# Five moves in the first two segments of a fused recurrence, MLP and MoE kernel: a buffer of its own and a sooner load for the first triangles' columns, weight conversions behind the first triangles, router steps and early scans in another place

## The chip, the cores and the metric

The kernel runs on one core of a Trainium2 chip. The metric is the time of one execution on the device, in microseconds (us); lower is better. TensorE (PE) does the matrix multiplications and the transpositions that go through PSUM, VectorE (DVE), ScalarE (ACT) and GpSimd (POOL) do elementwise work, and SyncE (SP) issues most of the DMA transfers. Each engine executes its own instructions in order, and waits for others through semaphores.

## The reference

Three stages follow one another: a recurrence over 768 time steps for 4 x 8 heads of 40 dimensions, an MLP with a squared ReLU on its 3072 x 320 output, and a mixture of 8 experts, of which each token takes one, with 768 places per expert.

```python
for t in range(S):                               # S = 768, 32 heads, D = 40
    y[:, :, t] = einsum('bhd,bhde->bhe', rt, state)
    Sa = einsum('bhde,bhe->bhd', state, at)
    state = state * wt[:, :, None, :] - einsum('bhd,bhe->bhde', Sa, bt)
    state = state + einsum('bhd,bhe->bhde', vt, kt)
...
x = np.maximum(x @ w_in, 0.0)                    # x 3072x320, w_in 320x2048
x = (x * x) @ w_out                              # w_out 2048x320
...
logits = x @ w_gate                              # 320x8
expert_idx = np.argmax(logits, axis=1)
h = np.maximum(np.einsum('ecd,edf->ecf', disp, w1), 0.0)   # disp 8x768x320
y = np.einsum('ecf,efd->ecd', h, w2)
out[i] = gate_w[i] * y[expert_idx[i], pos[i]]
```

## The kernel before

**The recurrence** (class `Rwkv`) is cut into 12 segments `s` of 64 steps, and each segment into two chunks `c` of 32 steps. Within a chunk the 32 dependent steps are turned into a triangular system. For one segment:

- `scale(s)` loads the decays `w_d` and the keys `kb_d`, takes running products of the decays (two scans, to `rq_r` and back into `w_d`, L127 and L140), multiplies `kb_d` by the first (L158), loads the columns `rq_a` (L163), multiplies them by the second (L167), and `place` writes them by DMA into the tiles `a` (L177). `products` has the scans; `g` is a copy of a few of their columns.
- `lower(s, c)` multiplies `kb_d` with `rq_a` on PE (tile `pa`), and ACT and DVE copy and mask the result (`sad_ab`, `am`, and its transposition to `a`, L213).
- `invert(s)` transposes the triangles on DVE (`solve_al`, L220) and then inverts them on POOL in 31 steps of two operations, `tmp` and `tl` (L333).
- `inverted(s)` transposes the inverse on DVE (`solve_tf`, L242) and adds its two halves into `tt`.
- `steps(s)` scans `wl` and transposes it to `rt` and `qt`. The state update of a chunk follows: `pr`, `psa`, `psd`, `ppq`, `pn` (the new state) and `py`, `pz` on PE, `zv` on DVE, and copies on ACT.

The tiles `solve_al` and `solve_tf` share one buffer (the tag before the dot in their names). So do `rq_r` and the columns `rq_a`, both named `rq16`: the load of `rq_a` therefore starts after the last reader of `rq_r`.

**The MLP** (class `Mlp`) runs beside the recurrence. Its float64 weights come as pairs of 32-bit words and are converted: `load_out(n)` makes one of 16 tiles of `w_out` (from the `stage` tiles; `ao`, `woh`, `lo`), `load_in(fp, k)` one of 20 blocks of `w_in` (`raw`, then `a`, `wi_hi`, `wi_lo`; the blocks of the third row group have `mh` and `ml`, and go to `wi_mx` by DMA). `from_double` is one ACT operation and three on DVE (L565 to L567); the remainder `lo`, `wi_lo` or `ml` is a subtraction in `less`, which for a few tiles is on POOL (L572) and else on DVE (L574). A block `raw` takes one of two tags with a few buffers. `routers` multiplies the gate into `w_out` (`ptg`, `wt`, `pog`, `wogl`). `add_y` turns a finished segment into `x_hi`, `x_lo` and `x_mx`, and `bursts` runs the MLP itself on it: `pl` (L494), `g`, `gh`, `gl` (L715), `acc` (L677).

**What sets the order.** The main loop goes through the segments and chunks, and each chunk through eight slots. After each slot, `mlp(n)` takes `n` pieces of the queue (first router steps, then bursts); the numbers stand in `FIRST` for segment 0, `SECOND` for segment 1 and `SLOTS` from segment 2 on. A scheduler orders the instructions of each engine by priority; within `high_priority` blocks they go ahead of the others. `issue_after(i)` puts what is issued in it behind instruction `i`: `behind(n)` behind the first `n` additions of the state update (`sums`), and `gated()` behind the list `gate` while `steady` holds, which is from segment 2 on. `gate` is the last `solve_al` and the `x_mx` of `add_y`. Before the loop stand `scale(0)`, four calls of `load`, `lower(0)` and `invert(0)`, the other calls of `load`, `steps(0)` and `scale(1)`.

## Time and profile before

| | |
|---|---|
| median of the runs | 1017.08 us (3 runs, 1012.47 to 1021.44) |
| profiled execution | 1013.06 us |
| its span | 1011.2 us |
| mean granted TensorE clock | 0.986 |
| busy PE / DVE / ACT / POOL | 877.8 / 744.1 / 620.0 / 540.0 us |
| chain that ended last | PE 31%, POOL 26%, DVE 13%, DMA 11%, issue 11%, ACT 5% |
| segments 0 to 11 | up to about 660 us; after it the rest of the MLP and the experts |

The profiled execution is 4.0 us shorter than the median. "Busy" counts the time in which an engine executes something; 31% in the chain's row says that this share of the span lies on the chain of work that was followed back from the last instruction, on that engine. The two lines of the inversion on POOL (`tl` and `tmp`, L333) are 13% and 12% of the span there.

### The profile page before, as it was taken

The numbers are of one execution on the slowest core, as the hardware profiler recorded it, in microseconds if no ns is written. First come the engines' busy times: TensorE is split into PE (matmuls) and PEld (weight loads), VectorE is DVE, ScalarE is ACT, GpSimd is POOL, SyncE is SP. The second block draws the span as 40 slices with busy tenths as digits, with TensorE's granted clock in tenths as the row PEclk, the third lists the DMA queues.
The fourth block names the chain that finished last, engine by engine and source line by source line (L and its number), as shares of the span: only waits on it lengthen the run. The fifth ranks groups of instructions, "written<-read, shape, count | busy, mean of one in ns | idle before, by whom it ended". The sixth has DMA issues, their size and how long they took to land.

```text
span 1011.2 us, 38777 instructions
## 1 busy us (share of the span) xinstructions
PE 877.8 (87%) x15962; PEld 824.2 (82%) x15962; DVE 744.1 (74%) x1657; ACT 620.0 (61%) x1618; POOL 540.0 (53%) x863
## 2 busy tenths in 40 slices
PE   1066666999998999999999999998899999999992
PEld 1055555898898999989998898998899889999992
DVE  7879698478777687878788775646569778888860
ACT  2144555566665767667666676664775577777750
POOL 4885759278777768787877878300000332323310
PEclk9999999999998999999999999999999999999997
DMA  7583653856655656656565655541882777777710
GB/s 218 167 286 93 179 168 115 289 150 174 175 173 158 181 162 187 176 175 177 177 183 176 187 164 150 144 133 56 262 257 76 225 208 235 219 230 233 232 48 10
DMA packets 91213, 177.17 MB, mean 175 GB/s; under 512 B 16490, under 2 KB 46828, under 8 KB 90061
## 3 DMA queue, kind: packets, MB, share of 16 engines
q1 hardware_dynamic: 87196, 164.99, 55.8%
q0 software_dynamic: 2880, 8.98, 2.8%
q8 instruction: 129, 2.11, 0.9%
q10 hardware_dynamic: 944, 0.57, 0.3%
q14 instruction: 64, 0.52, 0.2%
HBM read 138.52 MB, written 16.24 MB: 153 GB/s over the span
## 4 chain that ended last, share of the span: by engine, by line
PE 31%; POOL 26%; DVE 13%; DMA 11%; issue 11%; ACT 5%; SPq 1%; POOLq 0%; DVEq 0%; ACTq 0%
POOL tl L333 13%; POOL tmp L333 12%; PE pl L494 8%; PE acc L677 7%; PE upl L494 5%; PE uacc L1205 4%; DMA out_dram<-uo,room 4%; DMA xg<-x_dram,room 2%; DMA wol<-wol 1%; DVE rq_r L127 1%; PE pn L336 1%; DMA kb_d<-in_kb_dram 1%; PE ppq L336 1%; DVE solve_al L220 1%; DVE solve_tf L242 1%
## 5 line engine op out<-in xcount | busy, mean ns | idle before, releaser
L333 POOL TENSOR_TENSOR tmp<-solve_al,tl 128x126 f32<-128x126 f32 (+22 forms) x372 | 218.8, 588 | 74.5 <-DVE solve_al L220 46.3
L333 POOL TENSOR_TENSOR tl<-tl,tmp 128x126 f32<-128x126 f32 (+22 forms) x372 | 224.1, 602 | 29.0
L677 PE MATMUL acc<-woh,gh 128*128 128x328 f32 x384 | 127.9, 339 | 2.2 <-ACT x L739 2.2
L677 PE MATMUL acc<-wol,gh 128*128 128x328 f32 x384 | 119.3, 317 | 2.1 <-DMA wol<-wol 1.8
L494 PE MATMUL pl<-x_hi,wi_hi 128*128 128x256 f32 x384 | 116.0, 302 | 0.0
L1213 POOL DMA_INDIRECT xg<-x_dram,room x30 | 32.6, 1087 | 155.7 <-DVE x_lo L509 69.5
L494 PE MATMUL pl<-x_lo,wi_hi 128*128 128x256 f32 x384 | 109.3, 285 | 6.5 <-DVE x_lo L509 6.2
L494 PE MATMUL pl<-x_hi,wi_lo 128*128 128x256 f32 x384 | 108.9, 284 | 0.0
L1289 POOL DMA_INDIRECT out_dram<-uo,room x30 | 33.7, 1125 | 133.1 <-DVE uo L1278 79.4
L700 ACT ACTIVATE g<-pl 128x512 f32<-128x512 f32 x96 | 57.4, 598 | 72.3 <-PE pl L494 67.8
L715 DVE TENSOR_TENSOR gl<-g,gh 128x512 fp32r<-128x512 f32 x96 | 67.2, 700 | 37.0 <-ACT gh L704 36.5
L677 PE MATMUL acc<-woh,gl 128*128 128x328 f32 x384 | 90.0, 315 | 0.6 <-issue 0.6
L494 PEld LDWEIGHTS pl<-x_lo,wi_hi 128*128 128x128 f32 x384 | 73.3, 191 | 6.5 <-DVE x_lo L509 6.5
L677 PEld LDWEIGHTS acc<-woh,gh 128*128 128x128 f32 x384 | 72.9, 190 | 6.8 <-ACT x L739 2.4
L1205 PE MATMUL uacc<-w2h,hh 128*128 128x320 f32 x240 | 75.1, 313 | 3.4 <-ACT wi_hi L1161 2.7
L494 PEld LDWEIGHTS pl<-x_hi,wi_hi 128*128 128x128 f32 x384 | 73.0, 190 | 3.6
L677 PEld LDWEIGHTS acc<-wol,gh 128*128 128x128 f32 x384 | 73.4, 191 | 2.6 <-DMA wol<-wol 2.0
L1205 PE MATMUL uacc<-w2h,hl 128*128 128x320 f32 x240 | 74.5, 310 | 0.0
L1205 PE MATMUL uacc<-w2l,hh 128*128 128x320 f32 x240 | 74.3, 309 | 0.0
L494 PEld LDWEIGHTS pl<-x_hi,wi_lo 128*128 128x128 f32 x384 | 73.3, 191 | 0.4 <-issue 0.4
L336 PE MATMUL pa<-kb_d,rq_a 40*32 40x64 f32 x1536 | 31.3, 241 | 46.4 <-DVE rq_a L167 45.5
L336 PEld LDWEIGHTS pa<-kb_d,rq_a 40*32 40x32 f32 x1536 | 27.3, 123 | 50.6 <-DVE rq_a L167 45.7
(264 smaller groups left out, 2685.8 us busy)
## 6 DMA issues: line engine op xcount, KB each, us to landing
wol<-wol SPq DMA_DIRECT2D x96, 328.0 KB
w<-in_w_dram SPq DMA_DIRECT2D x30, 640.0 KB
w<-in_w_dram SPq DMA_DIRECT2D x30, 512.0 KB
zv<-in_vt_dram SPq DMA_DIRECT2D x48, 208.0 KB
kb_d<-in_kb_dram SPq DMA_DIRECT2D x24, 320.0 KB
tk<-in_tok_dram SPq DMA_DIRECT2D x24, 320.0 KB
rx<-rt SPq DMA_DIRECT2D x192, 40.0 KB
zk<-tk SPq DMA_DIRECT2D x48, 160.0 KB
```

The costliest lines, as they stand in the source:

```text
L127: nc.vector.tensor_tensor_scan(out=rf[:, ::-1], data0=w[:rows, 1:][:, ::-1], data1=seed, initial=0.0, op0=ALU.mult, op1=ALU.add)
L220: i = nc.vector.transpose(out=al.rearrange("p s t -> p (s t)"), in_=self.ab.rearrange("p s c h -> p s (c h)")[:, :, None].to_broadcast([12 ...
L242: nc.vector.transpose(out=tf.rearrange("p t u c h -> p (t u c h)"), in_=tl[:, :, :, None].to_broadcast([128, C, C // 2, 2]))
L333: self.last = f(*a, **k).ins
L336: self.tc.keep_in_program_order(self.nc.tensor.matmul(*a, **k))
L494: tc.keep_in_program_order(tc.nc.tensor.matmul(out, lhsT=a, rhs=b, start=n == 0, stop=n == len(seq) - 1))
L677: self.tc.keep_in_program_order(self.nc.tensor.matmul(*a, **k))
L700: nc.scalar.activation(g, pl, AF.Relu)
L715: i = self.nc.vector.tensor_tensor(out=p[4], in0=g, in1=gh.bitcast(F32), op=ALU.subtract)
L1205: self.tc.keep_in_program_order(self.nc.tensor.matmul(*a, **k))
L1213: nc.gpsimd.indirect_dma_start(out=xg[:, 0:DX], out_offset=None, in_=self.x1, in_offset=bass.IndirectOffsetOnAxis(ap=self.idx[2 * j + t], ...
L1289: self.nc.gpsimd.indirect_dma_start(out=self.out, out_offset=bass.IndirectOffsetOnAxis(ap=self.to[:, n:n + 1], axis=0), in_=o[:, t], in_of ...
```

## The change

The diff has five parts. (1) The columns `rq_a` of segment 0 get the tag `solve`, which `solve_al` has, and their load is issued inside the first step of `scale(0)`. (2) All calls of `load` stand behind the first `lower` and `invert`, and the first DVE operation of each conversion is issued after the first `solve_al` (`hold`). (3) `solve_tf` of segments 0 and 1 is not put behind the state update any more. (4) All 34 router pieces are taken in segment 0; before, six were left for segment 1, and they have other slots now. (5) `steady` holds from segment 1 on.

```diff
@@ -149,7 +149,10 @@
             nc.sync.dma_start(out=w[BY_COL[j]], in_=src["wd"][s, j])
         for j in range(2):
             nc.sync.dma_start(out=kb[BY_COL[j]], in_=src["kb"][s, j])
-
+        x = None
+        if s == 0:
+            x = self.tile([128, NC, 16, C], f"rq16.a{s}", 1, tag="solve")
+            nc.sync.dma_start(out=x[:ROWS].rearrange("p c n t -> p (c n t)"), in_=src["ad"][s])
         yield
         pr = self.products(w, 16, ROWS, s)
         with self.gated():
@@ -159,8 +162,9 @@
         g = self.tile([128, 16], f"g64.{s}", 2)
         nc.vector.tensor_copy(g[:ROWS], r[:ROWS, :, 0])
         self.pre[s] = [g, [None] * NC, None]
-        x = self.tile([128, NC, 16, C], f"rq16.a{s}", 1)
-        nc.sync.dma_start(out=x[:ROWS].rearrange("p c n t -> p (c n t)"), in_=src["ad"][s])
+        if x is None:
+            x = self.tile([128, NC, 16, C], f"rq16.a{s}", 1)
+            nc.sync.dma_start(out=x[:ROWS].rearrange("p c n t -> p (c n t)"), in_=src["ad"][s])
         yield
         q = next(pr)
         yield
@@ -238,7 +242,7 @@
 
         nc, tl = self.nc, self.tl
         tf = self.tile([128, C, 2, NC, H], f"solve.tf{s}", 1)
-        with self.behind(1):
+        with self.behind(s > 1):
             nc.vector.transpose(out=tf.rearrange("p t u c h -> p (t u c h)"),
                                 in_=tl[:, :, :, None].to_broadcast([128, C, C // 2, 2]))
         tt = self.tile([128, C, NC, H], f"tt.{s}", 1)
@@ -538,6 +542,7 @@
         self.gl = w.tile([128, NFT, NEXP], F32R, name="wogl")
         self.wg = w.tile([128, 3, NEXP], F32, name="wg")
 
+        self.hold = self.first = None
         self.tops = [w.tile([128, self.NT], F32R, name=f"tops{i}") for i in range(2)]
         self.turned = 0
         for t in self.tops:
@@ -562,7 +567,8 @@
         V = nc.vector
         af = a.bitcast(F32)
         nc.scalar.activation(af, up.bitcast(F32), AF.Abs, scale=2.0 ** -112)
-        V.tensor_scalar(out=a, in0=a, scalar1=0x07ffffff, scalar2=3, op0=ALU.bitwise_and, op1=ALU.logical_shift_left)
+        with self.tc.issue_after(self.hold) if self.hold is not None else ExitStack():
+            V.tensor_scalar(out=a, in0=a, scalar1=0x07ffffff, scalar2=3, op0=ALU.bitwise_and, op1=ALU.logical_shift_left)
         V.scalar_tensor_tensor(out=a, in0=up, scalar=0xc0000000, in1=a, op0=ALU.bitwise_and, op1=ALU.bitwise_or)
         V.scalar_tensor_tensor(out=a, in0=low, scalar=29, in1=a, op0=ALU.logical_shift_right, op1=ALU.bitwise_or)
         return af
@@ -1392,9 +1398,8 @@
 TURN_AT = 2
 FAR = 1e6
 SLOTS = (2, 2, 3, 2, 2, 2, 3, 2), (2, 2, 3, 2, 2, 1, 1, 1)
-LEAD = 4
 SECOND = (2, 2, 2, 2, 2, 2, 2, 2), (2, 2, 2, 2, 2, 2, 2, 0)
-FIRST = (16, 0, 0, 0, 0, 0, 2, 2), (2, 2, 2, 2, 0, 0, 0, 0)
+FIRST = (14, 2, 0, 0, 0, 0, 2, 2), (0, 0, 4, 2, 2, 2, 2, 2)
 
 ORDER = list(range(NFT))
 for _n in range(4):
@@ -1452,14 +1457,14 @@
         with tc.high_priority(offset=2 * AHEAD):
             for _ in rw.scale(0):
                 pass
-        load(ORDER[:LEAD])
         with tc.high_priority(offset=2 * AHEAD):
             rw.lower(0, 0)
             rw.lower(0, 1)
             rw.invert(0)
+            ml.hold = rw.gate[-1]
             rw.put()
             rw.put()
-        load(ORDER[LEAD:])
+        load(ORDER)
         with tc.high_priority(offset=AHEAD):
             for _ in rw.steps(0):
                 pass
@@ -1587,7 +1592,7 @@
                         rw.lower(s + 2, 1)
                         rw.put(True)
 
-                rw.steady = s > 1
+                rw.steady = s > 0
                 parts = slot_a, slot_r, slot_b, slot_c, slot_d, slot_e, slot_f, slot_g
                 if c == 1:
                     parts = slot_a, slot_r, slot_b, slot_d, slot_f, slot_g, slot_h, slot_i
```

The next fences show how the engines' orders stand before and after, with the lines of each kernel. First DVE before the change, around the first `solve_al` (the third row from the end); `pa` and `sad_ab` are the products of segment 0, the rows with `ao` conversions of `w_out`.

```order
L201 TENSOR_TENSOR am_0_339<-pa_0_202,ct_106 128x256
L566 SCALAR_TENSOR_TENSOR ao_190<-stage_lo,ao_190 128x320
L565 TENSOR_SCALAR ao_352<-ao_352 128x320
L567 SCALAR_TENSOR_TENSOR ao_170<-stage_hi,ao_170 128x320
L567 SCALAR_TENSOR_TENSOR ao_180<-stage_mx,ao_180 128x320
L213 STREAM_TRANSPOSE a_114<-am_0_339 64x8x32 x2
L567 SCALAR_TENSOR_TENSOR ao_190<-stage_lo,ao_190 128x320
L566 SCALAR_TENSOR_TENSOR ao_352<-stage_hi,ao_352 128x320
L220 STREAM_TRANSPOSE solve_al_270<-sad_ab_201 128x1024
L201 TENSOR_TENSOR am_1_345<-pa_1_236,ct_106 128x256
L567 SCALAR_TENSOR_TENSOR ao_352<-stage_hi,ao_352 128x320
```

And DVE after it, at the same place. `w_d` and `rq_r_734` here belong to segment 1.

```order
L124 MEMSET seed_q 104x16
L205 TENSOR_TENSOR am_0_299<-pa_0_162,ct_106 128x256
L127 SCALAR_TENSOR_TENSOR rq_r_734<-w_d,seed_q 104x1040
L217 STREAM_TRANSPOSE a_114<-am_0_299 64x8x32 x2
L129 TENSOR_SCALAR rq_r_734<-rq_r_734 104x1040
L224 STREAM_TRANSPOSE solve_al_230<-sad_ab_161 128x1024
L571 TENSOR_SCALAR ao_312<-ao_312 128x320
L571 TENSOR_SCALAR ao_322<-ao_322 128x320
L205 TENSOR_TENSOR am_1_305<-pa_1_196,ct_106 128x256
L137 RECIPROCAL seed_q<-rq_r_734 104x16
```

The conversions stand behind `solve_al` now, and the scan of segment 1's decays (L127) and the clamp of its result (L129) ahead of it.

On POOL, this stands ahead of the first step of the first inversion before the change.

```order
L572 ISA
L572 TENSOR_TENSOR lo_166<-ao_160,woh 128x320
L572 TENSOR_TENSOR lo_176<-ao_170,woh 128x320
L572 TENSOR_TENSOR lo_186<-ao_180,woh 128x320
L572 TENSOR_TENSOR lo_196<-ao_190,woh 128x320
L333 TENSOR_TENSOR tmp_273<-solve_al_270,tl_272 128x31
```

After the change the first four subtractions stand within the inversion; here are the first two, in its eighth and ninth steps.

```order
L337 TENSOR_TENSOR tmp_233<-solve_al_230,tl_232 128x96
L578 TENSOR_TENSOR lo_318<-ao_312,woh 128x320
L337 TENSOR_TENSOR tl_232<-tl_232,tmp_233 128x24x4
L578 TENSOR_TENSOR lo_328<-ao_322,woh 128x320
L337 TENSOR_TENSOR tmp_233<-solve_al_230,tl_232 128x115
```

The four `lo` have moved from ahead of the inversion into it (the other two stand at its twelfth step, alike).

On DVE in segment 1, before the change, this stands ahead of `x_lo` of the first MLP tile; `kb_d`, `g_3` and `w_d` are those of segment 3.

```order
L457 TENSOR_TENSOR wogl<-pog,woh 128x8
L158 TENSOR_TENSOR kb_d<-kb_d,rq_r_1959 104x1024 x2
L160 COPY g_3_1965<-rq_r_1959 104x16
L140 SCALAR_TENSOR_TENSOR w_d<-w_d,seed_q 104x1040
L574 TENSOR_TENSOR wi_lo<-a_0_634,wi_hi 128x256
L574 TENSOR_TENSOR wi_lo<-a_0_652,wi_hi 128x256
L509 TENSOR_TENSOR x_lo<-pt,x_hi 128x8x32
L510 TENSOR_TENSOR x_mx<-pt,tops_100 64x4x32
```

After the change the same stretch reads as follows.

```order
L397 TENSOR_TENSOR zv_116<-zv_116,g_1_740 40x8x2x40 x2
L513 TENSOR_TENSOR x_lo<-pt,x_hi 128x8x32
L514 TENSOR_TENSOR x_mx<-pt,tops_100 64x4x32
L391 TENSOR_TENSOR rq_a_1294<-rq_a_1294,g_2_1292 104x512
L306 TENSOR_TENSOR tk_0_1548<-tk_0_1548,rx_0_1554 128x2x8x40
L124 MEMSET seed_q 104x16
L127 SCALAR_TENSOR_TENSOR rq_r_1981<-w_d,seed_q 104x1040
L129 TENSOR_SCALAR rq_r_1981<-rq_r_1981 104x1040
L137 RECIPROCAL seed_q<-rq_r_1981 104x16
L161 TENSOR_TENSOR kb_d<-kb_d,rq_r_1981 104x1024 x2
L163 COPY g_3_1987<-rq_r_1981 104x16
L140 SCALAR_TENSOR_TENSOR w_d<-w_d,seed_q 104x1040
```

`x_lo` and `x_mx` stand ahead of the two scans and the multiplication of `kb_d` now, and the first `gl` behind them; before, the first `gl` came later than all rows shown.

On SP, in segment 0's second chunk, the writes to `wi_mx` and the loads of `raw` stand like this before the change.

```order
L617 DMA wol_96<-lo_470 128x320
L603 DMA wi_mx<-mh_520 64x256
L603 DMA wi_mx<-ml_521 64x256
L603 DMA wi_mx<-mh_520 64x256
L603 DMA wi_mx<-ml_521 64x256
L559 DMA raw_0_528<-in_w_in_dram 128x512
L559 DMA raw_1_537<-in_w_in_dram 128x512
L559 DMA raw_0_546<-in_w_in_dram 128x512
L559 DMA raw_1_555<-in_w_in_dram 128x512
```

After the change they stand in this order.

```order
L564 DMA raw_1_537<-in_w_in_dram 128x512
L181 DMA a_114<-rq_a_1294 40x512 x2
L258 DMA wl_2087<-in_wl_dram 128x651
L564 DMA raw_2_564<-in_w_in_dram 64x512
L609 DMA wi_mx<-mh_520 64x256 x2
L564 DMA raw_0_546<-in_w_in_dram 128x512
L564 DMA raw_2_564<-in_w_in_dram 64x512
L609 DMA wi_mx<-ml_521 64x256 x2
L564 DMA raw_0_580<-in_w_in_dram 128x512
```

Four loads of `raw` stand ahead of the first `wi_mx` write now (the first of them seven rows ahead of this piece), and the others alternate with it.

## Rows read from the trace of the kernel before

**Rows 1.** Windows cut at `solve_al` starts: bounds, length, each engine's busy us (instructions), clock.

```profile
86.40:141.30 54.90, 38.26 (x856) 32.60 (x856) 45.83 (x115) 29.53 (x90) 35.37 (x67) 1.00 0.60 174
141.30:206.40 65.10, 50.71 (x1133) 45.90 (x1134) 45.46 (x87) 36.24 (x92) 39.51 (x67) 0.97 0.62 194
...
409.80:458.50 48.70, 47.94 (x1165) 44.34 (x1164) 39.24 (x68) 33.78 (x80) 38.65 (x65) 1.00 0.61 178
```

**Rows 2.** Timeline of DVE, the first triangles and their inverse: start, duration, instruction, [idle, releaser].

```profile
8.69 2.33 DVE L127 TENSOR_TENSOR_SCAN rq_r<-w_d,seed_q 104x1040 f32<-104x1040 f32 x1 [3.69 <-DMA w_d<-in_wd_dram]
...
19.59 1.23 DVE L167 TENSOR_TENSOR rq_a<-rq_a,w_d 104x1024 f32<-104x1024 f32 x1 [0.29 <-DMA rq_a<-in_ad_dram]
...
31.16 1.23 DVE L220 STREAM_TRANSPOSE solve_al<-sad_ab 128x1024 f32<-128x1024 f32 x1
...
34.79 2.32 DVE L127 TENSOR_TENSOR_SCAN rq_r<-w_d,seed_q 104x1040 f32<-104x1040 f32 x1
...
76.52 1.25 DVE L242 STREAM_TRANSPOSE solve_tf<-tl 128x1024 f32<-128x1024 f32 x1 [2.80 <-POOL tl L333]
```

**Rows 3.** Timeline of SP's DMA issues, the first 31 us.

```profile
2.31 0.28 SPq L149 DMA_DIRECT2D w_d<-in_wd_dram  x1
...
14.87 0.32 SPq L163 DMA_DIRECT2D rq_a<-in_ad_dram  x1
...
20.84 3.16 SPq L177 DMA_DIRECT2D a<-rq_a  x4
...
29.33 0.90 SPq L149 DMA_DIRECT2D w_d<-in_wd_dram  x2
```

**Rows 4.** Timeline of POOL, ahead of the first inversion and in it.

```profile
26.23 1.18 POOL L572 TENSOR_TENSOR lo<-ao,woh 128x320 fp32r<-128x320 f32 x1 [14.53 <-ACT woh L614]
28.97 2.99 POOL L572 TENSOR_TENSOR lo<-ao,woh 128x320 fp32r<-128x320 f32 x3 [1.55 <-ACT woh L614]
...
34.81 2.41 POOL L333 TENSOR_TENSOR tl<-tl,tmp 128x58 f32<-128x58 f32 x1
...
52.19 0.41 POOL L333 TENSOR_TENSOR tmp<-solve_al,tl 128x126 f32<-128x126 f32 x1
52.67 0.56 POOL L333 TENSOR_TENSOR tl<-tl,tmp 128x126 f32<-128x126 f32 x1
```

**Rows 5.** Timeline of DVE, segment 0's second chunk: the first and last of four waits.

```profile
118.30 0.42 DVE L509 TENSOR_TENSOR x_lo<-pt,x_hi 128x256 fp32r<-128x256 f32 x1 [2.35 <-ACT x_mx L508]
...
125.24 0.29 DVE L565 TENSOR_SCALAR a<-a 128x256 uint32<-128x256 uint32 x1 [0.59 <-ACT a L564]
125.45 0.42 DVE L567 SCALAR_TENSOR_TENSOR a<-raw,a 128x256 uint32<-128x256 uint32 x1
125.78 0.42 DVE L574 TENSOR_TENSOR wi_lo<-a,wi_hi 128x256 fp32r<-128x256 f32 x1
```

**Rows 6.** Timeline of PE in segment 1, up to the first MLP products.

```profile
144.29 1.29 PE L336 MATMUL pr<-zv,a 104*32 104x40 f32 x64 [2.33 <-ACT wt L629]
...
154.31 0.56 PE L307 MATMUL pz<-ct,zv 40*104 40x40 f32 x7 [2.64 <-DVE wogl L457]
154.81 1.54 PE L677 MATMUL pog<-wg,wt 128*128 128x8 f32 x6
156.28 0.58 PE L494 MATMUL pl<-x_hi,wi_hi 128*128 128x256 f32 x1
163.10 0.58 PE L494 MATMUL pl<-x_lo,wi_hi 128*128 128x256 f32 x1 [6.23 <-DVE x_lo L509]
```

**Rows 7.** Timeline of DVE in segment 1, beside and behind Rows 6.

```profile
150.32 1.81 DVE L393 TENSOR_TENSOR zv<-zv,g 40x640 f32<-40x640 f32 x2
...
156.66 2.64 DVE L158 TENSOR_TENSOR kb_d<-kb_d,rq_r 104x1024 f32<-104x1024 f32 x2 [2.40 <-DMA kb_d<-in_kb_dram]
...
159.53 2.31 DVE L140 TENSOR_TENSOR_SCAN w_d<-w_d,seed_q 104x1040 f32<-104x1040 f32 x1
...
172.42 0.72 DVE L715 TENSOR_TENSOR gl<-g,gh 128x512 fp32r<-128x512 f32 x1 [0.71 <-ACT gh L704]
```

## The prediction

> **What bounds the kernel now.** I read the windows cut at the starts of `solve_al` first, since every segment has one such start and its spacing is the segment's price. From segment 3 on a segment takes about 49 us, with PE busy for 47.94 of 48.70: there PE is the bound, at full clock. The two windows from 86.40 to 206.40 take 54.90 and 65.10 us, and no engine is full in either: PE is busy for 38.26 and 50.71, DVE for 45.83 and 45.46 [rows 1]. So the change can win or lose in the first three segments only, and what it wins there arrives at the end as a shift, if PE's order behind them stays.
>
> Next come the waits in these windows. In segment 1 PE starts the first MLP product at 156.28 and then stands for 6.23 us until `x_lo` is there at 163.10 [rows 6]. In the order of DVE the row ahead is `kb_d`'s multiplication, which itself waited 2.40 us for its load, and the second scan [rows 7]. In segment 0, DVE waits four times between 118.30 and 125.24, for 2.35, 1.69, 1.08 and 0.59 us, 5.7 in all [rows 5]: the blocks `raw` of `w_in` come late, because on SP they stand behind writes to `wi_mx`, whose `ml` a subtraction on POOL makes between two steps of the inversion.
>
> Last come the first triangles. `rq_a` is multiplied at 19.59, when its load lands; `solve_al` starts at 31.16, and POOL's inversion fills the time until `solve_tf` at 76.52, which waits for it. From 31.16 to 76.52 the path is POOL alone [rows 2].
>
> **Part 1 and the first triangles.** The sooner load lets the multiplication of `rq_a` follow the decay scan at about 17.1 instead of 19.59: 2.5 us sooner for `pa` and `sad_ab`. But in DVE's order `solve_al` now stands behind the scan of segment 1's decays. Their load goes out behind the four writes of `a`, which take 3.16 us: `rq_a` is done at 18.3 (17.1 and 1.23), the writes at 21.5, and the two `w_d` issues by 22.4 (0.90) [rows 2, 3]. How long they take to land no row shows; the nearest are `rq_a`, issued at 14.87 and waited for until 19.59 (4.7 us), and `w_d` of segment 0, issued at 2.31 and waited for until 8.69 (6.4 us, with the whole start of the kernel beside it) [rows 2, 3]. I take 4.9, near the one that is nearer in time: the scan starts at 27.3, costs 2.3 [rows 2], and 0.9 for a transposition and 0.7 for the clamp follow. `solve_al` then starts at 31.2, against 31.16: **nothing won**, with ends of -1.1 (21.5 and 4.7) and +1.5 (22.4 and 6.4). The fourteen conversions that stood there on DVE before were the reason for the late start; the scan takes their place.
>
> **Part 2, inside the first inversion.** Four `lo` subtractions, 1.18 and 2.99 us, stood ahead of the inversion on POOL, in time that it had to wait anyway; now they stand in it [rows 4], where each delays the end: **+4.2 us**. Against that, POOL's `tl` of 128x58 took 2.41 us beside the scan on DVE that began at 34.79 [rows 2, 4], where even the larger 128x126 takes 0.41; this scan is ahead of the inversion now: **-2.0**. The conversions that moved from ahead of it put nine more DVE operations with two SBUF inputs beside it. A POOL step beside such a row took 0.56 instead of 0.41 (at 52.67, beside a merge of words; 52.19 was free) [rows 4]; 0.15 each and nine of them make 1.3, of which I take **1.2**, for not each meets a POOL step. The sum for `solve_tf(0)` and so for `solve_al(1)` is **+3.4**.
>
> The Trainium skill, on the page "SBUF — State Buffer" under "Who interferes with whom", says that a DVE instruction with two SBUF inputs contends with a GpSimd instruction that reads SBUF, and that the shared pair is an exclusive lock. By that rule each of the nine could hold POOL for its full length, 3.8 us instead of 1.2 at the 0.42 of such a row, and the sum below would be -4.7 instead of -7.3. The row at 52.67 speaks for less, the one at 34.81 for the full lock.
>
> **Parts 2 and 4, from `solve_al(1)` to `solve_al(2)`.** The `w_in` conversions that segment 1 had, and the last router steps, come in here. Counting DVE's order, this stretch gets ten more word merges, five masks, four `wi_lo` and an `ml`, three `wogl` and the mask of a triangle, and loses a `lo`, an `rq_a` and two `tk`. At the pitch of rows such as 125.45 and 125.78 (0.33 apart) and 0.21 for a mask [rows 5], that is **+4.8 us** of DVE, of which none need be on the path, since DVE has 9.1 us of idle time in this window (54.90 less 45.83 [rows 1]); I take all, for most of that idle time is waits that the path goes through. Four loads of `raw` now stand ahead of the first `wi_mx` write on SP, which takes the reason from most of the 5.7 us: I take **-4.0**, between 0 and -5.7. Together +0.8, and `solve_al(2)` stands +4.2 later, at 145.5.
>
> Part 3 frees `solve_tf(0)` and `(1)` of an ordering behind the state update. `solve_tf(0)` waits for POOL [rows 2] and has no update ahead of it; `solve_tf(1)` had the inverse ready some 12 us before it ran, at 135.56. It can now run sooner and take 2 us of DVE work (1.23 and 0.7) off the busy end of segment 0. But what follows it, `pa` of the next triangles, waits for other things too: priced at nothing, with an end of -2.
>
> **Parts 4 and 5, segment 1.** Here lies the gain. Relative to `solve_al(2)`, PE started the first MLP product at +15.0 (156.28 less 141.30). The routers' share of that goes: 2.33 us of waiting for `wt`, 2.64 for `wogl`, and a product `pog` of 1.54 [rows 6], which leaves +8.5. DVE has only `solve_al`, transpositions, `y` and `zv` (1.81 [rows 7]) ahead of `x_lo`, 4.9 us in all, so it isn't what ends last; the wait of 6.23 goes as well. The second product, at +21.8 before, then comes at +9.1: **-12.7 us** (2.33 + 2.64 + 1.54 + 6.23). The scans that stood ahead now stand between `x_lo` and the first `gl`. That `gl` ran 9.3 us behind the resumed products (172.42 less 163.10 [rows 6, 7]), so it is due at +18.4; DVE gets to it after 2.3 for each scan, 2.64 for `kb_d`, 0.7 for the clamp and some 3 us of smaller ones, 11 us behind +8.5, at +19.6: **+1.2**. That counts on `kb_d`'s load being there; before, its multiplication waited 2.40 us for it, and on SP its issue keeps its place behind three `wol`.
>
> POOL's second inversion is late by the +4.2, too, but from segment 3 on PE is the bound, and `solve_tf` of segments 4 and 5 had some us to spare for POOL: nothing.
>
> **The sum.** +3.4 + 0.8 - 12.7 + 1.2 = -7.3 us. The profiled execution of 1013.06 becomes 1005.8. It stands 4.0 below the median of the runs shown, so I forecast 1009.8, say **1010 us**.
>
> **The rivals.** *A larger gain.* The raw blocks' stall goes entirely (-1.7 more), the decays of segment 1 land early (-1.1), `solve_tf(1)` brings its -2, and the nine conversions hold POOL for nothing (-1.2): -13.3, or about 1004 us. For it speaks that DVE's rows in segment 0 have few other waits; against it, that four ends must come together.
>
> *No change.* The nine conversions block POOL for their whole time (9 times 0.42 [rows 5], +2.6 over my 1.2), as the whole scan was paid for at 34.81 [rows 4], and the stall of the blocks stays (+4.0): -0.7, or about 1016 us. Against it, a step beside such a row took 0.15 more and not 0.42.
>
> *Slower.* On SP the remaining loads of `raw` alternate with the `wi_mx` writes of the group before, so each of the three `w_in` groups still to come could cost the 5.7 us stall within segment 0 instead of beside MLP work in segment 1, where PE used to have other things to do. Then the stretch from `solve_al(1)` to `solve_al(2)` grows by 4.8 + 17.1 instead of 0.8, the sum is 3.4 + 21.9 - 12.7 + 1.2 = +13.8, and the median about 1031 us. It decides from the point where that stretch takes more than 63 us (54.90 and 8.1), since only 8.1 us of later gain pay for it. Against it: SP has four loads ahead, and the buffers for `raw` alternate between two tags.
>
> **How the numbers follow.** Forecast 0.48, larger gain 0.27, no change 0.14, slower 0.11. One per cent, 10 us, is about what a measurement of this kernel can tell from no change. The median must be under 1006.9 for faster: about a quarter of the forecast's case (0.13) and nearly four fifths of the larger gain's (0.21) lie there, so faster has 0.34; slower has the 0.11 of its rival; the rest, 0.55, is within 1%. For the range I leave out the slower rival and the far end of the larger gain: the forecast's unknown ends, -1.1 to +1.5 for the start, some 3 for POOL and 4 for the blocks, give 999 to 1020.
>
> **What would show it.** In the changed profile: `solve_al(0)` starting at about 31, behind a scan; the first inversion some 3 us longer, with four `lo` in it; `solve_al(2)` at about 145; `x_lo` no longer the releaser of a 6 us wait in PE's first `pl`; `solve_al` starts some 49 us apart from segment 3 on. The prediction is wrong if the stretch from `solve_al(1)` to `solve_al(2)` swells, if the first `gl` makes PE wait for much more than 1.2 us (a late `kb_d` would), or if later segments lose their pace by PE's order or a lower granted clock.

## The result, and the profile after

The changed kernel is slower: 1024.25 us median (1021.39 to 1030.25, 17 runs) against 1019.16 us (1010.97 to 1024.98, 17 runs), a ratio of 1.0074 with a 95% interval of 1.0053 to 1.0095, some 7.5 us. The medians alone are 5.1 us apart; I go by the ratio throughout. A run more than 1.5% above the fastest of its kernel counts as slow and is left out of the ratios. The forecast was 7 us the other way. The loss is under the one per cent that the prediction took for the least that can be told, but clear of its interval. The profiled execution took 1026.99 us, above its median by 2.7, while the one before lay 6.1 below that of its 17 runs; so of the 13.9 us between the two spans about half is the change, and I compare starts within segments rather than ends.

The windows of the changed kernel, cut at `solve_al` of segments 0 to 4, answer to [rows 1].

```profile
30.78:88.76 57.98, 23.58 (x325) 20.00 (x326) 46.85 (x86) 21.30 (x63) 44.83 (x69) 1.00 0.69 208
88.76:148.58 59.82, 41.10 (x920) 36.09 (x922) 52.94 (x136) 33.35 (x105) 31.17 (x68) 1.00 0.56 164
148.58:206.77 58.19, 48.81 (x1099) 44.16 (x1091) 38.90 (x67) 32.23 (x76) 37.05 (x65) 0.94 0.56 177
206.77:260.78 54.01, 48.09 (x1129) 43.84 (x1129) 38.88 (x66) 30.86 (x74) 38.56 (x65) 0.91 0.64 173
```

The second row is the first loss: 59.82 instead of 54.90, with DVE busy for 52.94 instead of 45.83. The third is 58.19 instead of 65.10, which looks like the forecast gain; but the fourth takes 54.01 where the kernel before took 49.00, and the granted clock of both is 0.94 and 0.91. A `solve_al` start doesn't say how far PE is. The starts of `pr`, one per chunk, do, but only from segment 2's second chunk on: at segment 2's first (213.48, before 208.35) the changed kernel has done twelve more `acc` products, with no router steps left for segment 1; from the second chunk's on, PE has done the same number of instructions in both. That `pr` starts at 238.19 (before 232.32), the one of segment 4 at 314.52 (308.13). So the way from `solve_al(2)` to that `pr` gave back 1.4 of the 7.3 us by which `solve_al(2)` was late, and not 11.5.

The first triangles on DVE, with the first inversion's subtractions on POOL, answer to [rows 2, 4].

```profile
10.63 2.33 DVE L127 TENSOR_TENSOR_SCAN rq_r<-w_d,seed_q 104x1040 f32<-104x1040 f32 x1 [5.63 <-DMA w_d<-in_wd_dram]
...
18.53 1.23 DVE L171 TENSOR_TENSOR rq_a<-rq_a,w_d 104x1024 f32<-104x1024 f32 x1
...
27.00 2.32 DVE L127 TENSOR_TENSOR_SCAN rq_r<-w_d,seed_q 104x1040 f32<-104x1040 f32 x1 [1.21 <-DMA w_d<-in_wd_dram]
...
30.78 1.24 DVE L224 STREAM_TRANSPOSE solve_al<-sad_ab 128x1024 f32<-128x1024 f32 x1
...
79.14 1.25 DVE L246 STREAM_TRANSPOSE solve_tf<-tl 128x1024 f32<-128x1024 f32 x1 [0.74 <-POOL tl L337]
```

```profile
43.25 1.10 POOL L578 TENSOR_TENSOR lo<-ao,woh 128x320 fp32r<-128x320 f32 x1
44.91 0.93 POOL L578 TENSOR_TENSOR lo<-ao,woh 128x320 fp32r<-128x320 f32 x1
...
48.95 2.84 POOL L337 TENSOR_TENSOR tl<-tl,tmp 128x126 f32<-128x126 f32 x1
...
52.21 1.31 POOL L578 TENSOR_TENSOR lo<-ao,woh 128x320 fp32r<-128x320 f32 x1
53.88 0.85 POOL L578 TENSOR_TENSOR lo<-ao,woh 128x320 fp32r<-128x320 f32 x1
```

With the load of `rq_a` third on SP, the first scan is late: 10.63 instead of 8.69, behind a wait of 5.63 for `w_d` instead of 3.69. It starts at 10.2 to 10.7 in all seventeen profiles with part 1 and at 8.5 to 8.7 in the three without. Of the 2.5 us meant for `rq_a` 1.1 is left (18.53 for 19.59). `solve_al` is 0.4 sooner, and `solve_tf` 2.6 later, with the four `lo` (4.2 us) in the inversion.

PE in the second chunk of segment 0 and in segment 1, against [rows 6]:

```profile
130.80 0.72 PE L311 MATMUL pz<-ct,zv 40*104 40x40 f32 x8 [3.60 <-ACT woh L460]
...
155.43 0.58 PE L498 MATMUL pl<-x_hi,wi_hi 128*128 128x256 f32 x1 [1.26 <-ACT x_hi L510]
156.31 0.58 PE L498 MATMUL pl<-x_lo,wi_hi 128*128 128x256 f32 x1 [0.31 <-DVE x_lo L513]
...
170.44 0.59 PE L683 MATMUL acc<-woh,gl 128*128 128x328 f32 x2 [4.46 <-DVE gl L721]
...
210.18 0.64 PE L683 MATMUL acc<-wol,gh 128*128 128x328 f32 x1 [3.94 <-DMA wol<-wol]
```

The wait of 6.23 us for `x_lo` is gone, as forecast: the second product runs 7.7 us behind `solve_al(2)` instead of 21.8. Two new waits stand in its place, 4.46 for `gl` and 3.94 for a load of `wol`. Earlier, in segment 0 at 130.80, PE waits 3.60 for a router step's copy on ACT. ACT had stood still for the blocks of `w_in`:

```profile
128.94 0.43 ACT L569 ACTIVATE a<-raw 128x256 f32<-128x256 f32 x1 [2.81 <-DMA raw<-in_w_in_dram]
```

The chain that leads to the wait for `gl` shows what I had not priced (start, us, what):

```profile
156.45 0.60 DVE rq_a L391
157.05 0.74 DVE tk L306
...
157.94 3.38 DMA a<-rq_a
...
161.44 2.34 DVE rq_r L127
163.80 0.73 DVE rq_r L129
...
164.72 2.52 DVE kb_d L161 x2
167.24 0.33 DVE g L163
167.57 2.23 DVE w_d L140
169.81 0.59 DVE gl L721
```

The scan writes into the buffer that `rq_a` has, so it waits until `rq_a`, just scaled by `g` on DVE, has gone out by DMA: 3.4 us in which DVE does nothing, and the first `gl` stands behind it. The wait for `wol` is read from SP's issues:

```profile
181.82 0.84 SPq L1414 DMA_DIRECT2D out_dram<-zero  x2
...
184.04 3.59 SPq L1414 DMA_DIRECT2D out_dram<-zero  x5
...
189.47 3.95 SPq L1414 DMA_DIRECT2D out_dram<-zero  x6
...
199.18 5.93 SPq L295 DMA_DIRECT2D rx<-rt  x8
...
207.03 1.68 SPq L687 DMA_DIRECT2D wol<-wol  x3
```

And before the change:

```profile
186.63 8.16 SPq L1409 DMA_DIRECT2D out_dram<-zero  x12
...
196.87 2.40 SPq L1612 DMA_DIRECT2D x_dram<-zero  x4
199.32 0.93 SPq L681 DMA_DIRECT2D wol<-wol  x2
```

In segment 1 SP writes zeros to the output (sixteen) and to the last rows of `x_dram` (four). Before, `wol` was issued right behind them, at 199.32. Now the later scan of `wl` has moved the eight `rx` among these writes, and `wol` is issued at 207.03. From 181.82 to 207.03 SP issues without a gap of more than 0.12 us, so `wol` stands behind the time that the issues ahead of it take, 5.93 us of it for the eight `rx`. The tile of zeros also keeps ACT's next `gh` waiting for its buffer, for 2.28 us until 208.68; that isn't PE's wait, since the `acc` product that waits for `wol` reads the `gh` that the product ahead of it, at 205.82, had read.

The granted clock fell in or right behind both new waits (windows of the changed kernel; the clock is the third number from the end):

```profile
165.00:170.00 5.00, 0.99 (x8) 0.72 (x6) 5.00 (x5) 0.55 (x1) 4.84 (x3) 1.00 0.47 146
170.00:175.00 5.00, 4.56 (x84) 4.07 (x85) 3.11 (x5) 2.60 (x6) 4.41 (x8) 0.59 0.28 89
...
205.00:210.00 5.00, 1.24 (x77) 0.86 (x65) 3.01 (x6) 2.66 (x6) 1.54 (x5) 0.84 0.63 195
210.00:215.00 5.00, 4.82 (x77) 4.39 (x78) 0.72 (x4) 0.15 (x2) 4.06 (x13) 0.50 1.00 269
```

0.50 is the lower of the two levels, 1.2 GHz of 2.4. The kernel before had 1.00 in these stretches, but went to the lower level once as well, between 195 and 200:

```profile
195.00:200.00 5.00, 5.00 (x80) 4.61 (x80) 2.47 (x5) 1.41 (x4) 0.00 (x0) 0.68 0.99 356
```

From the second product of segment 1 to `pr` of segment 2's second chunk PE has the same 1501 instructions, in the changed kernel and then before:

```profile
156.31:238.19 81.88, 70.99 (x1501) 65.29 (x1501) 55.15 (x85) 42.36 (x99) 58.62 (x93) 0.90 0.61 183
163.10:232.32 69.22, 66.12 (x1501) 60.86 (x1501) 46.84 (x81) 41.53 (x97) 42.84 (x72) 0.98 0.61 185
```

The stretch is 12.7 us longer: 7.8 of it PE is idle, in the main for `gl` and `wol`, and 4.9 it is busy longer with the same work. With the 7.3 us from `solve_al(2)` and the 14.1 that the second product is sooner, this makes the 5.9 at that `pr`.

### The profile page after: what moved, and what is told of

Read it like the earlier page. It is cut to its first block, busy times and chain, and to the rows that moved or that the text cites. A ratio compares the mean times of both kernels' runs of the same rounds, so it can differ in the third digit from the quotient of the medians.

```text
span 1025.1 us, 38777 instructions
## 1 busy us (share of the span) xinstructions
PE 886.3 (86%) x15962; PEld 832.3 (81%) x15962; DVE 745.0 (73%) x1657; ACT 620.0 (60%) x1618; POOL 533.8 (52%) x863
## 4 chain that ended last, share of the span: by engine, by line
PE 30%; DMA 27%; DVE 18%; issue 14%; ACT 6%; SPq 3%; POOL 2%; POOLq 0%; DVEq 0%; ACTq 0%
PE pl L498 9%; PE acc L683 8%; DMA out_dram<-uo,room 6%; DMA wol<-wol 3%; DVE rq_r L127 3%; DMA rq_a<-in_ad_dram 3%; DMA a<-rq_a 2%; DMA kb_d<-in_kb_dram 2%; PE upl L498 2%; PE pa L340 2%; DMA lr<-in_rv_dram 2%; PE pn L340 2%; DVE kb_d L161 1%; DMA w_d<-in_wd_dram 1%; ACT sad L409 1%
## 5 line engine op out<-in xcount | busy, mean ns | idle before, releaser
L683 PEld LDWEIGHTS acc<-woh,gl 128*128 128x128 f32 x384 | 66.6, 193 | 4.7 <-DVE gl L721 4.7
```

The source lines that it names most:

```text
L683: self.tc.keep_in_program_order(self.nc.tensor.matmul(*a, **k))
```

## The experiments

All ratios are to the kernel before, with 12 runs of each kernel, 6 of e5b and of the four with the zeros spread, and 17 of the changed one. "Without" means the changed kernel with that part undone. The columns are: the ratio with its 95% interval, the stretch from `solve_al(1)` to `solve_al(2)`, and the start of `pr` of segment 2's second chunk and of segment 4 in the one profile of each.

| kernel | ratio | al(1) to al(2) | pr(2, second) | pr(4) |
|---|---|---|---|---|
| before | 1 | 54.9 | 232.3 | 308.1 |
| changed | 1.0074 [1.0053, 1.0095] | 59.8 | 238.2 | 314.5 |
| e1_no5: without 5 | 1.0001 [0.9969, 1.0033] | 63.4 | 232.4 | 308.2 |
| e3_no4: without 4 | 1.0000 [0.9968, 1.0032] | 55.7 | 235.1 | 309.1 |
| e8_no45: without 4 and 5 | 0.9971 [0.9936, 1.0006] | 54.4 | 228.8 | 304.1 |
| e4_no2: without 2 | 1.0033 [1.0001, 1.0066] | 56.8 | 234.7 | 310.0 |
| e5a: 5 in the first chunk only | 1.0051 [1.0023, 1.0079] | 61.1 | 240.9 | 315.5 |
| e5b: 5 in the second chunk only | 1.0124 [1.0088, 1.0160] | 62.7 | 237.7 | 312.4 |
| e8_lo: e8_no45, `lo` on DVE | 1.0022 [0.9995, 1.0048] | 58.2 | 231.6 | 306.5 |
| e12_clear: changed, zeros in segment 4 | 1.0049 [1.0025, 1.0074] | 60.8 | 232.9 | 308.7 |
| e17_3clear: e3_no4, zeros in 4 | 0.9948 [0.9918, 0.9978] | 56.5 | 228.2 | 303.3 |
| e16_13clear: e8_no45, zeros in 4 | 1.0027 [1.0002, 1.0053] | 54.9 | 230.6 | 305.4 |
| e15_bclear: before, zeros in 4 | 1.0069 [1.0036, 1.0103] | 57.1 | 234.8 | 310.3 |
| e19_spread: changed, zeros spread | 1.0209 [1.0154, 1.0265] | 60.6 | 233.0 | 321.2 |
| e18_3spread: e3_no4, zeros spread | 1.0195 [1.0140, 1.0250] | 56.7 | 226.9 | 310.8 |
| e21_8spread: e8_no45, zeros spread | 1.0205 [1.0147, 1.0262] | 54.8 | 230.6 | 317.4 |
| e20_bspread: before, zeros spread | 1.0219 [1.0163, 1.0274] | 54.3 | 231.4 | 318.6 |
| e23_late: changed, zeros behind segment 11 | 1.0041 [1.0009, 1.0073] | 59.8 | 231.2 | 307.2 |
| e22_3late: e3_no4, zeros behind segment 11 | 0.9979 [0.9943, 1.0016] | 54.9 | 225.5 | 299.4 |

### One part undone

**Without part 5.**

```diff
-                rw.steady = s > 0
+                rw.steady = s > 1
```

> The changed kernel without part 5 (steady from segment 2 on again, so that segment 1's scans are not behind add_y). Theory A (the later scans cost as much as they free): the two new waits of PE in segment 1, 4.46 us for the first gl and 3.94 us for a wol load, go away, and the wait for x_lo of some 6 us comes back; pr of segment 2 starts within 2 us of 213.5 and the time is within 3 us of the changed kernel. Rival B (part 5 is the whole loss): x_lo does not wait, since the router steps are gone from segment 1, pr of segment 2 starts at 206 or sooner, and the time is 8 us under the changed kernel.

The time is 7.4 us under the changed kernel, so rival B's, but not by its reason: `x_lo` is late (165.78, with a wait of 2.33 us), `solve_al(2)` is at 152.77, later still, and both new waits are gone. Theory A's claim that part 5 costs as much as it frees fell: it costs 7 us more.

**Without part 4.**

```diff
-FIRST = (14, 2, 0, 0, 0, 0, 2, 2), (0, 0, 4, 2, 2, 2, 2, 2)
+FIRST = (16, 0, 0, 0, 0, 0, 2, 2), (2, 2, 2, 2, 0, 0, 0, 0)
```

> The changed kernel without part 4 (FIRST as before, six router pieces left for segment 1). Theory A (the crowding of segment 0's second chunk is by the router steps, whose PE products wait for ACT behind conversions): solve_al(1) to solve_al(2) falls from 59.8 to 56 us or less, and the time is 2 to 4 us under the changed kernel. Rival B (it is by the conversions alone, whose raw loads alternate with wi_mx writes on SP): that stretch stays at 59 to 60 us, and the router waits return in segment 1, so that the time is 2 to 5 us above the changed kernel.

The stretch falls to 55.7, as theory A said, and the time by 7.5 us, more than it said.

**Without both.**

> The changed kernel without parts 4 and 5, so parts 1 to 3 alone. Theory A: solve_al(1) at 88 to 89 as in the changed kernel (four lo in the first inversion), solve_al(1) to solve_al(2) at 56 us or less, segment 1 as in the kernel before with x_lo waiting some 6 us; 2 to 4 us above the kernel before. Rival B (the conversions' new place is the whole loss): solve_al(2) at 148 or later, and 7 us or more above the kernel before.

Both edits above together. Parts 1 to 3 alone come out at 0.9971, 3 us under the kernel before with an interval that just holds 1, where theory A had 2 to 4 us above, and `x_lo` makes PE wait for 1.54 us, not some 6. From the four kernels: part 4 costs 7.5 us with part 5, and part 5 as much with part 4; without the other each costs 3, which the intervals don't tell from nothing or from 7.5.

**Without part 2.**

```diff
+        load(ORDER[:4])
         with tc.high_priority(offset=2 * AHEAD):
             rw.lower(0, 0)
...
-            ml.hold = rw.gate[-1]
...
-        load(ORDER)
+        load(ORDER[4:])
```

> The changed kernel without part 2 (the first four load calls ahead of the first triangles again, no hold). Theory A: solve_al(0) some 1 us later, the four lo ahead of the first inversion, so solve_al(1) at 86 to 87 instead of 88.8; the crowding in segment 0's second chunk stays (59 to 60 us), and the time is 2 us under the changed kernel. Rival B (the conversions' place makes the crowding too): the stretch falls to 55 us and the time is 6 us or more under the changed kernel.

Between the two: the stretch falls to 56.8 and the time by 4 us. `solve_al(1)` stays late, at 89.70, for two of the four `lo` stand in the first inversion here too. So, with one kernel to show for part 2 by itself, the crowding of segment 0's second chunk takes both, the router steps of part 4 and the conversions that part 2 has pushed back: with both, the stretch is 59.8 to 63.4 in seven profiles; wherever one or both are missing, 54.3 to 58.2. Parts 1 and 3 were not undone by themselves.

### Part 5 by halves

This is e5a, with the first chunk's half; e5b has `c == 1` there.

```diff
-                rw.steady = s > 0
+                rw.steady = s > 1 or (s == 1 and c == 0)
```

> The changed kernel with part 5 only for the first chunk of segment 1 (its scan of the decays w_d stands behind add_y, the scan of wl in the second chunk does not). Theory A (the first scan makes the first gl late, the second scan sends eight rx transfers on SP ahead of the wol load): the wait of 4.5 us for gl stays, the wait of 3.9 us for wol falls under 1 us, pr of segment 3 starts at 259 to 261 instead of 262.9, 3 to 5 us under the changed kernel. Rival B (the wol wait has another reason, such as the later pace of the bursts): both waits stay, and the time is within 2 us of the changed kernel.

> The changed kernel with part 5 only for the second chunk of segment 1. Theory A: the first scan is early again, so solve_al(2) is late (151 to 153) and gl makes PE wait for under 1 us, but the wol load still makes it wait for some 3 to 4 us; the time is 2 to 5 us above the changed kernel without part 5, so 2 to 5 us under the changed kernel. Rival B (only the first scan's place costs): no wol wait, as fast as the changed kernel without part 5.

The wait for `gl` goes with the first half, as theory A said (4.36 in e5a, none in e5b; in all twenty profiles it is there just where the first half is, 1.7 to 4.5 us). The wait for `wol` does not go with the second: e5b has it, and e5a too, longer than the changed kernel. The times were missed: e5a is 2.3 us under the changed kernel, which the intervals don't separate, and its `pr` of segment 3 starts at 266.0; e5b is 5 us above it, where both theories had it under. So the halves don't add up to part 5, and why the second alone costs most is not shown. PE of e5a:

```profile
208.10 0.64 PE L683 MATMUL acc<-wol,gh 128*128 128x328 f32 x1 [7.14 <-DMA wol<-wol]
```

In e5a `rx` goes out before the zeros; there the zeros themselves start later, at 190.98 instead of 181.82, and `wol` behind them at 204.19. My sentence on `rx` was too narrow. What the kernels with a wait share is the block of zero writes with something that came late ahead of or among it: five profiles have part 5 or a half of it and the twenty zeros in segment 1, and PE waits for `wol` there, 2.3 to 7.1 us; in the other fifteen it does not.

### The zero writes

First the twenty writes were moved to segment 4, in four kernels.

```diff
-                if s == 1 and c == 0:
+                if s == 4 and c == 0:
                     zero = ml.tile([128, 480], "zero", "gh", 2)
                     clear(nc, zero, out)
```

> The changed kernel with the twenty zero writes (out and the end of x_dram) issued in segment 4 instead of segment 1. Theory A (in the second chunk of segment 1 the wol loads stand on SP behind these writes and behind rx, which part 5 pushed among them): the wait of 3.9 us for wol goes to under 0.5, the low clock right behind it goes too, pr of segment 3 starts at 256 to 259 instead of 262.9, and the time is 4 to 6 us under the changed kernel. Rival B (the burst's pace or rx alone): wol still waits 3 us or more, and the time is within 2 us of the changed kernel.

> The kernel before, with the zero writes in segment 4. Theory A: the kernel before has no wol wait in segment 1, so nothing is won: within 2 us. Rival B (the writes slow the DMA of segment 1 in any kernel): 3 us or more faster.

> The changed kernel without parts 4 and 5, with the zero writes in segment 4. Theory A: it has no wol wait either, so within 2 us of that kernel, some 3 us under the kernel before. Rival B: 3 us or more under that kernel.

> The changed kernel without part 4, with the zero writes in segment 4. Theory A: its wol wait of 2.3 us and the low clock behind it go, 2 to 4 us under the changed kernel without part 4, so as much under the kernel before. Rival B: the wait goes, but the time stays, as another wait takes its place.

At `pr` of segment 2's second chunk the changed kernel is 5.3 us sooner and the one without part 4 6.8, while the two controls are 1.8 and 2.5 later. So there theory A holds, and the wait for `wol` is gone in both. In the end the move costs every kernel something new, in segment 4, where `zk` now stands behind the block; before with its zeros moved, PE:

```profile
359.12 1.10 PE L336 MATMUL pn<-zv,zk 64*40 64x40 f32 x18 [4.04 <-DMA zk<-tk]
```

The controls lose 5.7 and 7.0 us by it; the kernels with part 5 come out 2.5 and 5.3 faster in spite of it, the 2.5 within the intervals and under the 4 to 6 that theory A had. The one without part 4 has the lowest ratio of the study, 0.9948. Its interval overlaps with those of e8_no45 and e22_3late, and the medians of all its runs and the kernel before's, 1014.73 and 1018.00, make 0.9968: that it is the fastest isn't shown.

Then I spread the writes, four at a time, over segments 2 to 6.

```diff
-                if s == 1 and c == 0:
-                    zero = ml.tile([128, 480], "zero", "gh", 2)
-                    clear(nc, zero, out)
...
+                if 2 <= s < 7 and c == 0:
+                    zero = ml.tile([128, 480], f"zero{s}", "gh", 2)
+                    nc.vector.memset(zero, 0.0)
...
+                    for n in range(4 * (s - 2), 4 * (s - 1)) if s < 6 else ():
+                        nc.sync.dma_start(out=ov[n], in_=zero)
```

> The changed kernel without part 4, with the zero writes four at a time in segments 2 to 6 instead of all twenty in segment 1. Theory A (twenty writes in a row on SP hold up whatever stands behind them: the wol load in segment 1 if part 5 has put rx among them, zk in segment 4; four at a time hold up nothing): no wait of PE for wol or zk over 1 us, 5 us or more under the same kernel with the writes in segment 4, so 10 us or more under the kernel before. Rival B (the writes cost their time wherever they stand): as that kernel, 5 us under the kernel before.

> The changed kernel with the zero writes four at a time in segments 2 to 6. Theory A: neither the wol wait of 3.9 us nor the zk wait of 4.3 us; 6 to 10 us under the changed kernel, so about as the kernel before, since part 4's crowding of segment 0 and the 4 us wait for gl are left. Rival B: within 3 us of the changed kernel.

> The kernel before with the zero writes four at a time in segments 2 to 6. Theory A: these writes held up nothing there in segment 1, so it is within 2 us of the kernel before. Rival B (the spread writes are worth something to any kernel): 4 us or more faster, and then the wol wait is not what part 5 costs.

> The changed kernel without parts 4 and 5, with the zero writes four at a time in segments 2 to 6. Theory A: within 2 us of that kernel with the writes in segment 1, 3 us under the kernel before, and slower than the one with part 5. Rival B: 4 us or more under it.

All four come out 2% slower, both theories' times missed. The tile of zeros has one of the two buffers of `gh`, and now holds it once in each of five segments; `gh`, and behind it on ACT `sa`, wait. Spread in the kernel before, ACT and PE:

```profile
242.50 0.62 ACT L704 CAST gh<-g 128x512 fp32r<-128x512 f32 x1 [5.87 <-DMA out_dram<-zero]
...
243.63 0.72 PE L307 MATMUL psd<-ct,sa 128*104 128x128 f32 x4 [3.46 <-ACT sa L374]
```

Up to there (`pr` of segment 2's second chunk) the picture is that of the move: 226.9 and 233.0 with part 5, controls within 2 us.

Last, the sixteen writes of the output behind segment 11.

```diff
+                if (s, c) in ((1, 0), (11, 1)):
...
+                    for n in range(16) if s == 11 else ():
+                        nc.sync.dma_start(out=ov[n], in_=zero)
```

> The changed kernel without part 4, with the sixteen zero writes of out behind the last chunk of segment 11 (the four of x_dram stay in segment 1). Theory A (the block of writes on SP is what turned part 5 into a loss): no wol wait in segment 1 and no zk or psd wait later, pr of segment 2's second chunk at 227 to 229 as with the writes in segment 4 or spread, instead of 235.1, kept to the end of segment 11: 8 to 12 us under the kernel before, if the writes hold up nothing in the expert weights' loads. Rival B (whatever has to wait behind the block there costs as much): the gain is there at segment 11 and gone at the end.

> The changed kernel with the same later zero writes. Theory A: pr of segment 2's second chunk at 233 instead of 238.2, and 4 to 7 us above the one without part 4, which is what the router steps in segment 0 cost; the end within 4 us of the kernel before. Rival B: as for the kernel without part 4, gone at the end.

Without part 4, segment 4 starts 8.7 us sooner than in the kernel before and the last segment 6.4 sooner (`pr` of segment 11 at 648.74 against 655.18), as theory A said; at the end 2.1 are left of the 8 to 12 forecast, within the interval. The sixteen issues take 9.99 us on SP, ahead of the experts' weights, ACT's `gh` waits 4.75 us for the zeros' buffer at 707.53, and PE waits 4.63 us for ACT at 723.51, for 2.28 at the same place before: rival B for a part. How large a part is open, since from the last `pr` to the end the profiles take anything from 330.9 to 338.4 us, with the same code there in all but the two kernels with late zeros (338.0 and 333.2). Part 4 (e23_late) costs 7.8 us on top at segment 4, and 6.3 in the time.

### The four subtractions

```diff
-POOLED_OUT = range(4)
+POOLED_OUT = ()
```

> The changed kernel without parts 4 and 5, and with the four lo subtractions of the first tiles on DVE instead of POOL. Theory A (each lo within the inversion delays its end by its length): the first inversion is 3 to 4 us shorter, solve_tf(0) at 75 to 76 instead of 78.6, solve_al(1) at 85 to 86 instead of 88.7, and the end 2 to 3 us sooner than the kernel without parts 4 and 5. Rival B (DVE's extra two-input operations hold POOL as long): solve_tf(0) stays at 78 or later, and nothing is won.

> The same kernel as the one with the four lo on DVE, once more: a second look at its profile, for how far the starts of solve_al and the granted clock differ between two executions of one kernel. Either theory expects the starts of solve_al(1) to (4) within 1 us of the first look's, and the low-clock stretches in the same places.

DVE in the first profile, the ends of the first two inversions and the start of `solve_al(1)` between them:

```profile
77.38 1.25 DVE L246 STREAM_TRANSPOSE solve_tf<-tl 128x1024 f32<-128x1024 f32 x1 [3.70 <-POOL tl L337]
...
86.64 1.23 DVE L224 STREAM_TRANSPOSE solve_al<-sad_ab 128x1024 f32<-128x1024 f32 x1
...
123.75 1.25 DVE L246 STREAM_TRANSPOSE solve_tf<-tl 128x1024 f32<-128x1024 f32 x1 [4.51 <-POOL tl L337]
```

The first inversion is 2.2 us shorter and, from a start 1.0 later, ends 1.2 us sooner, not 3 to 4, and `solve_al(1)` 2.1; none of it arrives, since the next stretch is 3.8 us longer and the time 5 us more than with `lo` on POOL. The end of the first inversion does not pass through to `solve_al(2)`. The second profile, of a single run (1015.59 us), has the starts of `solve_al(1)` to `(4)` within 1.8 us of the first, where 1 was expected: differences of such a size between two profiles say nothing. The low-clock stretches are not in the same places (0.51 from 141 to 165.5 us in the second, 1.00 there in the first), against what either theory expected.

## Why the prediction was wrong, step by step

- **First triangles, "nothing won".** 30.78 against the 31.2 forecast, but in part by luck. The sooner load delays the first scan by 1.9 us, which I had not seen, so the two `w_d` were issued by 23.9 and not by 22.4; they landed 3.1 us behind that and not 4.9, and the two errors make the scan of segment 1's decays start at 27.00 for a forecast 27.3.
- **First inversion, +3.4.** Measured +2.4 at `solve_al(1)`. That it would pass through to segment 1 as a shift is not borne out by e8_lo.
- **`solve_al(1)` to `solve_al(2)`, +0.8.** This step failed: +4.9. The term of +4.8 for more DVE work came out at 7.1 (52.94 less 45.83); I had taken the pitch of the quickest rows, 0.33 us, for merges that follow one another at some 0.43 there. The term of -4.0 for the stall of the `raw` blocks came out at -2.2, all that DVE's idle time shrank (6.9 for 9.1). And it could not have been more than 3.4: I misread the first of the four waits in [rows 5], 2.35 us for `x_lo`. ACT was not waiting for a block there; it made `x_mx` in its order behind other copies, and the blocks came later (before the change):

```profile
116.24 1.20 ACT L449 COPY zk<-pz 40x160 f32<-40x160 f32 x4
...
118.00 0.26 ACT L508 CAST x_mx<-pt 64x128 fp32r<-64x128 f32 x1
...
120.13 0.43 ACT L564 ACTIVATE a<-raw 128x256 f32<-128x256 f32 x1 [1.32 <-DMA raw<-in_w_in_dram]
```

In the changed kernel ACT still waited 2.81 us for a block, and the router steps of part 4, which I priced as a few `wogl` on DVE, made PE wait for ACT. That the place was that of my slower rival was right, its price (22 us) and its reason (SP alone) were not; the runs show it needs parts 2 and 4 together.
- **Part 3, nothing.** `solve_tf(1)` ran at 127.30 instead of 135.56, and `solve_al(2)` was later all the same.
- **The wait for `x_lo`, -12.7.** The size is right, 14.1, the reason only in part: 3.8 of it are there without parts 4 and 5 (the second product runs 18.0 us behind `solve_al(2)` in e8_no45, for 21.8 before), where that wait is 1.54 us for 6.23. Part 5 by itself makes the 18.0 into 10.3 and part 4 into 13.0.
- **The first `gl`, +1.2.** Mis-sized: 4.46. I counted DVE's rows behind `x_lo` and not that the scan waits for the DMA out of the buffer it writes (3.4 us).
- **What else part 5 moves.** This was missing altogether. I followed `x_lo` and `gl` and not the DMAs that follow the second scan on SP. The wait of 3.94 us for `wol` came from there, with the half clock behind it; with the block of zeros out of segment 1 the kernels with part 5 are 5 to 10 us sooner at segment 2's second chunk and the others are not sooner by more than 1 us.
- **"From segment 3 on a shift."** Only roughly: +4.7 at `pr` of segment 3, +6.4 at segment 4, +8.8 at segment 11, +13.9 at the end. The last 5 us are no more than profiles of the same code differ in that stretch.

That the time stayed within the one per cent to which I gave 0.55 is luck, too: it got there from the other side.

What stays open: how much of the lost time the half clock is. The 4.9 us that PE is busy longer with the same 1501 instructions are an estimate of it; three profiles at full clock (e1_no5, e8_lo, e15_bclear) have 64.4 to 65.3 us there, and the changed kernel 70.99. No run varied the clock alone, and none gave the scan a buffer of its own, which is what the wait for `gl` asks for. Nor do the times show that parts 4 and 5 cost more together than the sum of each: the 4.5 us between 7.5 and 3 have an uncertainty of some 6, and at `pr` of segment 2's second chunk part 4 costs 3.1 us with part 5 and 3.6 without.

## What to carry to other kernels

When instructions are put behind a point, list everything that hangs on them, the DMA issues on every queue too, and look at what stands behind these on the queue: a block of issues that just fitted before is where it will be lost. Before moving steps into a stage that "has room", look at the busy time of each engine in that stage; DVE had 9 us of 55 free and got 7 more. And check a gain at several points of the program on the engine that bounds the rest, since the start that one watches may only have moved past the wait.

## What the hardware showed that I had not expected

- The granted clock went to half in or right after a wait of PE of some 4 us in the midst of busy stretches (0.59 behind 4.46 us, 0.50 behind 3.94 us). In the kernel before a wait of 6.23 us, with less work ahead of it, had none behind it, and the 0.68 between 195 and 200 came behind a wait of 1.17 us: the length of the wait alone does not tell. Long stretches at half clock with a lightly busy PE (0.53 from 101 to 166 us in the profile of e8_no45) cost nothing that shows: its stretch from `solve_al(1)` to `solve_al(2)` took 54.36 us at 0.65 and 54.77 at 1.00 in e21_8spread, which is the same up to there.
- On POOL a `tl` step of 128x126 took 2.84 us (0.43 for the next of that shape, at 56.19), beside DVE's multiplication of `rq_a` (1.42 us) and two subtractions and a multiplication behind it. Before, the same step took 2.04 us, beside the same multiplication of `rq_a` (1.43 us, at 47.65) and one more behind it. The Trainium skill, page "SBUF — State Buffer", section "Who interferes with whom", has two-input DVE instructions contend with GpSimd's reads; these rows agree, and show that several of them in a row can hold one POOL step. A scan does the same: the four that fell into the first inversion before (2.3 to 2.5 us each) stood beside POOL steps of 2.2 to 2.5 us.
